# Middle phase of an FFT convolution: the inverse's two blocks together, one period later

## The chip, the cores and the metric

The kernel runs on one core of a Trainium2 chip. The metric is the device time of one execution in microseconds. The engines are TensorE (PE; its weight loads appear as PEld), VectorE (DVE), ScalarE (ACT), GpSimd (POOL) and SyncE (SP, which here only issues DMAs).

## The reference

For a batch of 4, a sequence of 12800 and 128 channels, in float32: a filter comes from a small network on position embeddings, times an exponential window; the product `x * v` is convolved with it along the sequence by FFT; the result times `x` goes through a causal convolution of five taps, a sigmoid gate and two 128x128 projections.

```python
h_filt = (np.maximum(pos_emb @ w1, 0.0) @ w2) * window
u = x * v
y = np.fft.irfft(np.fft.rfft(u, n=2*S, axis=1) * np.fft.rfft(h_filt, n=2*S, axis=0)[None], n=2*S, axis=1)[:, :S]
x = x * y
gate = 1 / (1 + np.exp(-causal_conv5(x, conv_w)))
out = (gate * (x @ w_val)) @ w_out
```

## The kernel before

The sequence is cut into J = 2 blocks of 6400 = N1 x N2 = 100 x 64 points, and the transform is done in two stages. The first phase transforms along the 100 (index `k1` afterwards) and writes `a_u` to memory. The middle phase takes one `k1` after the other, two at a time (a pair p of 0 to 49): it transforms along the 64, multiplies by the filter's spectrum, and does the first stage of the inverse, whose result `c_y` goes to memory. The last phase finishes the inverse, and does the gate and the projections.

The change is in the middle phase alone (lines 398 to 431). Its order is written out by hand: each engine does its work in the order of the code, and waits where a result, or a buffer, is not there yet. Turn p of the loop touches three pairs:

- `load_pair(p + 2)` issues the loads on SP (L354 for a table of weights, once per four pairs, and L359 for the signal). The tiles come from a pool `ld` of six buffers, where a load waits until the buffer's last reader is done.
- `spectrum(.., 1, 0)` and `(.., 1, 1)` of pair p: TensorE, L341, two matmuls each, 64 columns of the array wide ("column tiles"), into `z_ps`, a ring of four PSUM banks that the filter uses too.
- `times` (VectorE, L346) multiplies spectra by the filter: `va` and `vb` (2048 wide) and `vc` and `vd` (1024 wide).
- `inverse` (TensorE, L369) of pair p-1, for block 0 from `va` and for block 1 from `vc`, four matmuls each, with a contraction of 64 rows of the array ("row tiles"), into `c_ps`, two buffers. ScalarE copies each (L376), and after block 1 issues the two stores of `c_y` (L379).
- `start_pair(p + 1)` makes the filter of the next pair (TensorE L328, ScalarE L333 to L335). `first` and `second` are that pair's two spectra of block 0, for `va` and `vb` of the next turn.
- The add of L419 (VectorE) adds half of pair p-1's `va` to its `vc`; `inverse` of block 1 reads the sum.
- Three sums on GpSimd end the turn: L428 (`va[0:2] += vb[0:2]`), L429 (`vc += vd`), L430 (`va[2:4] += vb[2:4]`).

So in turn p VectorE does `va`, `vb`, the add for p-1, `vc`, `vd`. The add needs L429 and L430 of the turn before. L428 needs `vb` of its own turn, L429 needs `vd`. A spectrum's bank in `z_ps` is free again when VectorE has read it: `first` waits for the `vb` before, `second` for the `vc` before, and the pair of block 1 for the `vd` before and for ScalarE's copies of the filter.

Of the kernel before, what the change touches and what calls it, by code (L numbers as in the profile page):

```python
# [105 lines left out]
def tile_longconv_gate(  # L106
# [56 lines left out]
    def load():  # L163
        return ld.tile([128, 2048], F32, name="ld")
# [149 lines left out]
    with tc.tile_pool(name="p2", bufs=1) as p2, tc.tile_pool(name="ps2", bufs=1, space=PSUM) as ps2:  # L314
        BD = B * D
        NP = N1 // 2
        PG = KG // 2
        half = [slice(h * N2, (h + 1) * N2) for h in range(2)]

        def bank():  # L320
            return ps2.tile([128, BD], F32, name="z_ps", bufs=4)

        def filter_pair(p):

            h_ps = bank().rearrange("p (c e) -> p c e", c=2)
            for c in range(2):
                for h in range(2):
                    nc.tensor.matmul(  # L328
                        out=h_ps[half[h], c], lhsT=ag[:, 2 * p + h].rearrange("p j e -> p (j e)")[:, half[c]],
                        rhs=w2bd.rearrange("p j d -> p (j d)"), start=True, stop=True)  # L330
            h_sb = p2.tile([128, 2, J, 2, D], F32, name="h_sb2", bufs=3)
            src = h_ps.rearrange("p c (j d) -> p c j d", j=J)
            nc.scalar.copy(out=h_sb[:, 0].rearrange("p j c d -> p c j d"), in_=src)  # L333
            nc.scalar.activation(h_sb[:, 1, :, 0], src[:, 1], AF.Copy, scale=-1.0)
            nc.scalar.copy(out=h_sb[:, 1, :, 1], in_=src[:, 0])  # L335
            return h_sb

        def spectrum(a2, wk, j, c):
            z = bank()
            for h in range(2):  # L340
                nc.tensor.matmul(out=z[half[h]], lhsT=wk[:, h, half[c]], rhs=a2[:, h, j], start=True, stop=True)  # L341
            return z

        def times(out, z, h_sb, n):

            nc.vector.tensor_tensor(  # L346
                out, z.rearrange("p (b d) -> p b d", d=D).unsqueeze(1).to_broadcast([128, n, B, D]),
                h_sb.unsqueeze(2).to_broadcast([128, n, B, D]), op=ALU.mult)

        def load_pair(p):  # L350
            if p % PG == 0:
                n_p = min(PG, NP - p)
                wt = load().rearrange("p (k c e) -> p k c e", k=PG, c=4)
                nc.sync.dma_start(out=wt[:, 0:n_p], in_=t_w[:, p:p + n_p])  # L354
                weights.append(wt)
            a2 = load().rearrange("p (k j e) -> p k j e", k=2, j=J)
            step = 1 if p == 0 else 2
            for i in range(0, 2, step):
                nc.sync.dma_start(  # L359
                    out=a2[:, i:i + step].rearrange("p k j e -> p k (j e)"),  # L360
                    in_=a_u[2 * p + i:2 * p + i + step].rearrange("k c n j b d -> (c n) k (j b d)"))
            return a2, weights[-1][:, p % PG]

        def inverse(p, j, vt):
            wk = loaded[p][1]
            c_ps = ps2.tile([128, 2, BD], F32, name="c_ps", bufs=2)
            for c in range(2):
                for h in range(2):
                    nc.tensor.matmul(  # L369
                        out=c_ps[:, h], lhsT=wk[half[h], 2 + c], rhs=vt[half[h], c].rearrange("p b d -> p (b d)"),  # L370
                        start=(c == 0), stop=(c == 1))
            if j == 0:
                c_sb = p2.tile([128, 2, J, B, D], F32, name="c_sb", bufs=2)
                outs[p] = c_sb
            c_sb = outs[p]
            nc.scalar.copy(out=c_sb[:, :, j].rearrange("p h b d -> p h (b d)"), in_=c_ps)  # L376
            if j == J - 1:
                for h in range(2):
                    nc.scalar.dma_start(  # L379
                        out=c_y[:, 2 * p + h].rearrange("j p b d -> p j (b d)"),  # L380
                        in_=c_sb[:, h].rearrange("p j b d -> p j (b d)"))

        weights, loaded, outs = [], {}, {}
        filt_p, z0, v_p = {}, {}, {}
        AHEAD = 2

        def start_pair(p):
            filt_p[p] = filter_pair(p).rearrange("p s j c d -> p s (j c) d")

        def first(p):  # L390
            z0[p, 0] = spectrum(*loaded[p], 0, 0)

        def second(p):
            z0[p, 1] = spectrum(*loaded[p], 0, 1)

        with tc.manual_schedule():
            for p in range(-1, NP + 1):
                now, nxt, old = 0 <= p < NP, p + 1 < NP, 0 <= p - 1  # L400
                for q in range(AHEAD + 1) if p < 0 else (p + AHEAD,):
                    if q < NP and q not in loaded:
                        loaded[q] = load_pair(q)
                if now:
                    h = filt_p.pop(p)
                    z10 = spectrum(*loaded[p], 1, 0)
                    z11 = spectrum(*loaded[p], 1, 1)
                    va = p2.tile([128, 2 * J, B, D], F32, name="va", bufs=3)
                    vb = p2.tile([128, 2 * J, B, D], F32, name="vb", bufs=2)
                    times(va, z0.pop((p, 0)), h[:, 0], 2 * J)  # L410
                    times(vb, z0.pop((p, 1)), h[:, 1], 2 * J)
                if old:
                    oa, oc = v_p.pop(p - 1)
                    inverse(p - 1, 0, oa)
                if nxt:
                    start_pair(p + 1)
                    first(p + 1)
                if old:
                    nc.vector.tensor_tensor(oc, oc, oa[:, 2:4], op=ALU.add)  # L419
                    inverse(p - 1, 1, oc)  # L420
                if nxt:
                    second(p + 1)
                if now:
                    vc = p2.tile([128, 2, B, D], F32, name="vc", bufs=3)
                    vd = p2.tile([128, 2, B, D], F32, name="vd", bufs=2)
                    times(vc, z10, h[:, 0, 0:2], 2)
                    times(vd, z11, h[:, 1, 0:2], 2)
                    nc.gpsimd.tensor_tensor(va[:, 0:2], va[:, 0:2], vb[:, 0:2], op=ALU.add)  # L428
                    nc.gpsimd.tensor_tensor(vc, vc, vd, op=ALU.add)  # L429
                    nc.gpsimd.tensor_tensor(va[:, 2:4], va[:, 2:4], vb[:, 2:4], op=ALU.add)  # L430
                    v_p[p] = va, vc
# [234 lines left out]
```

## Time and profile before

| | us |
|---|---|
| Median of 3 runs | 1285.75 |
| Lowest and highest | 1273.37, 1292.47 |
| The profiled execution's time | 1290.03 |
| Its span, first to last instruction | 1288.2 |
| First phase | 0 to about 400 |
| Middle phase | about 400 to 850 |
| Last phase | about 850 to 1288 |

Over the span TensorE is busy for 1174.3 us (91%), VectorE for 1014.1 (79%), GpSimd for 867.4 (67%) and ScalarE for 629.6 (49%). Times in the rows of the timeline are the start in us from the span's start and the duration in us; in brackets stands how long the engine had been idle, and what ended that. In rows of groups stand the count, the busy time in us and the mean in ns, then the idle time before them. "x" and a number is how many instructions a row holds. A float32 matmul of the program appears as two instructions in the trace. TensorE's ends are modelled, so TensorE's times are best read from start to start.

### The profile page before, as it was taken

Reading aid. Unit: us, or ns where it says so; the run is one execution under the profiler, and the core shown is the slowest. Engines: PE = TensorE matmul, PEld = TensorE weight load, DVE = VectorE, ACT = ScalarE, POOL = GpSimd, SP = SyncE. Lnnn points to the kernel's source line nnn. Section 1 sums busy time; section 2 is a strip of 40 time slices with the busy share of each in tenths; the row PEclk is TensorE's granted clock in tenths of the full one; section 3 lists DMA queues with packets and bytes.
Section 4 is the critical chain, followed back from the end, with each engine's and each line's share of the span. In section 5 each row is a group of like instructions: output and inputs, shape, how many; then the busy total and the mean of one; then the engine's idle time right before and its main releaser. Section 6 shows DMA issues by size and latency. Waiting matters only on the chain.

```text
span 1288.2 us, 16767 instructions
## 1 busy us (share of the span) xinstructions
PE 1174.3 (91%) x5544; PEld 572.7 (44%) x5544; DVE 1014.1 (79%) x1130; ACT 629.6 (49%) x1064; POOL 867.4 (67%) x346
## 2 busy tenths in 40 slices
PE   4869999978777899999999999989999999999996
PEld 3557776766543233333333333353344444444432
DVE  5856233797655999999999999902999899999897
ACT  3324454677533233333333333304677677667664
POOL 3324233444543689999999999913898898898790
PEclk8979999988978999999999999986999999999999
DMA  9999878889988577788777777645888988999942
GB/s 244 293 298 311 240 238 270 275 259 304 297 260 306 199 263 282 275 286 293 279 278 278 276 276 258 246 142 154 250 270 269 287 255 274 285 272 268 285 142 102
DMA packets 152254, 332.95 MB, mean 258 GB/s; under 512 B 12446, under 2 KB 64714, under 8 KB 150634
## 3 DMA queue, kind: packets, MB, share of 16 engines
q1 hardware_dynamic: 104256, 226.13, 57.8%
q10 hardware_dynamic: 47914, 105.76, 22.7%
q8 instruction: 45, 0.74, 0.2%
q14 instruction: 39, 0.32, 0.1%
HBM read 200.77 MB, written 131.07 MB: 258 GB/s over the span
## 4 chain that ended last, share of the span: by engine, by line
PE 66%; DMA 16%; DVE 8%; issue 3%; POOL 3%; ACT 3%; SPq 1%; ACTq 0%; DVEq 0%; POOLq 0%
PE c_ps L369 14%; PE z_ps L341 13%; PE sd L503 8%; DMA ld<-in_v_dram 7%; PE o_ps L564 7%; PE fp L282 7%; DMA a_u<-st 6%; PE v_ps L554 5%; PE tp L517 4%; PE z_ps L328 3%; DVE gt L545 3%; PE ap L222 2%; PE ap L221 2%; PE o_ps L589 2%; DVE vc L419 1%
## 5 line engine op out<-in xcount | busy, mean ns | idle before, releaser
L530 POOL TENSOR_TENSOR ext<-yr,ld 128x400 f32<-128x400 f32 x120 | 301.6, 2514 | 60.4 <-DVE yr L528 40.5
L259 POOL TENSOR_TENSOR u_lo<-u_t,u_hi 100x1024 fp32r<-100x1024 f32 x64 | 160.0, 2503 | 236.1 <-ACT u_hi L258 212.2
L545 DVE SCALAR_TENSOR_TENSOR gt<-ext,cw,gt 128x1600 f32<-128x1600 f32 x128 | 242.7, 1896 | 0.9 <-ACT gt L542 0.8
L376 ACT COPY c_sb<-c_ps 128x1024 f32<-128x1024 f32 x100 | 101.2, 1012 | 278.4 <-PE c_ps L369 278.4
L341 PE MATMUL z_ps<-ld 128*64 128x512 f32 x800 | 195.3, 607 | 7.7 <-DMA ld<-a_u 6.5
L428 POOL TENSOR_TENSOR va<-va,vb 128x1024 f32<-128x1024 f32 x50 | 156.9, 3138 | 37.0 <-DVE vb L346 36.9
L282 PE MATMUL fp<-u_hi,fwd_hi 100*100 100x512 f32 x256 | 116.9, 456 | 57.5 <-ACT st L285 24.7
L503 PE MATMUL sd<-ld,inv 100*64 100x512 f32 x512 | 146.1, 645 | 2.4 <-DMA ld<-c_y 2.4
L287 DVE COPY st<-fp 100x512 f32<-100x512 f32 x128 | 85.3, 685 | 65.6 <-PE fp L282 57.9
L346 DVE TENSOR_TENSOR vb<-z_ps,h_sb 128x2048 f32<-128x2048 f32 x50 | 114.5, 2291 | 24.6 <-ACT c_sb L376 24.0
L564 PE MATMUL o_ps<-gd,wout 128*128 128x400 f32 x256 | 119.5, 548 | 13.8 <-DVE gd L559 9.4
L429 POOL TENSOR_TENSOR vc<-vc,vd 128x1024 f32<-128x1024 f32 x50 | 118.2, 2365 | 18.6 <-DVE vd L346 13.7
L257 DVE TENSOR_TENSOR u_t<-ld 100x1024 f32<-100x1024 f32 x64 | 86.2, 1348 | 51.7 <-POOL u_lo L259 42.3
L346 DVE TENSOR_TENSOR va<-z_ps,h_sb 128x2048 f32<-128x2048 f32 x50 | 114.1, 2281 | 10.9 <-PE z_ps L341 10.9
L510 ACT COPY sd_sb<-sd 128x512 f32<-128x512 f32 x128 | 75.8, 592 | 88.5 <-PE sd L503 73.6
L430 POOL TENSOR_TENSOR va<-va,vb 128x1024 f32<-128x1024 f32 x50 | 118.4, 2368 | 0.0
L369 PE MATMUL c_ps<-vc,ld 64*128 64x512 f32 x400 | 102.5, 631 | 11.0 <-DVE vc L419 10.6
L282 PE MATMUL fp<-u_hi,fwd_lo 100*100 100x512 f32 x256 | 108.8, 425 | 0.0
L554 PE MATMUL v_ps<-ext,wval 128*128 128x400 f32 x256 | 107.1, 500 | 0.0
L285 ACT COPY st<-fp 100x512 f32<-100x512 f32 x128 | 70.8, 592 | 73.2 <-PE fp L282 44.2
L341 PEld LDWEIGHTS z_ps<-ld 128*64 128x64 f32 x800 | 54.6, 138 | 114.2 <-issue 85.8
L258 ACT CAST u_hi<-u_t 100x1024 fp32r<-100x1024 f32 x64 | 68.2, 1067 | 74.0 <-PE fp L282 31.8
(78 smaller groups left out, 1962.0 us busy)
## 6 DMA issues: line engine op xcount, KB each, us to landing
c_y<-c_sb ACTq DMA_DIRECT2D x100, 512.0 KB
ld<-a_u SPq DMA_DIRECT2D x49, 1024.0 KB
ld<-c_y SPq DMA_DIRECT2D x128, 384.0 KB
ld<-in_xt_dram SPq DMA_DIRECT2D x32, 800.0 KB
out_dram<-o_sb ACTq DMA_DIRECT2D x32, 800.0 KB
ld<-in_x_dram SPq DMA_DIRECT2D x64, 384.0 KB
ld<-in_v_dram SPq DMA_DIRECT2D x64, 384.0 KB
a_u<-st ACTq DMA_DIRECT2D x64, 384.0 KB
```

The source lines that it names most:

```text
L259: nc.gpsimd.tensor_tensor(lo, u_t, hi.bitcast(F32), op=ALU.subtract)
L282: nc.tensor.matmul(out=fp, lhsT=w[:, c], rhs=d[:, b:b + 2], start=(k == 0), stop=(k == 2))
L341: nc.tensor.matmul(out=z[half[h]], lhsT=wk[:, h, half[c]], rhs=a2[:, h, j], start=True, stop=True)
L346: nc.vector.tensor_tensor(out, z.rearrange("p (b d) -> p b d", d=D).unsqueeze(1).to_broadcast([128, n, B, D]), h_sb.unsqueeze(2).to_broadc ...
L369: nc.tensor.matmul(out=c_ps[:, h], lhsT=wk[half[h], 2 + c], rhs=vt[half[h], c].rearrange("p b d -> p (b d)"), start=(c == 0), stop=(c == 1))
L428: nc.gpsimd.tensor_tensor(va[:, 0:2], va[:, 0:2], vb[:, 0:2], op=ALU.add)
L430: nc.gpsimd.tensor_tensor(va[:, 2:4], va[:, 2:4], vb[:, 2:4], op=ALU.add)
L503: nc.tensor.matmul(out=sd[c * N2:(c + 1) * N2], lhsT=inv[:, c], rhs=ct[c][:, r * B * D:(r + 1) * B * D], start=True, stop=True)
L530: nc.gpsimd.tensor_tensor(e[:, r0 + r], yr, xr, op=ALU.mult)
L545: nc.vector.scalar_tensor_tensor(gt, rows(t, k), cw[:, k:k + 1], gt, op0=ALU.mult, op1=ALU.add)
L554: nc.tensor.matmul(out=v_ps, lhsT=wval, rhs=rows(t)[:, r * ROW:(r + 1) * ROW], start=True, stop=True)
L564: nc.tensor.matmul(out=o_ps, lhsT=wout, rhs=gd, start=True, stop=True)
```

## The change

Both inverses of a pair stand together, in the turn after the one where the add was made, so two turns behind the pair's `va` and `vc`. `second` follows `first` at once. The add stays in its turn, now in a line of its own (L422). The loop has one turn more.

```diff
-            for p in range(-1, NP + 1):
-                now, nxt, old = 0 <= p < NP, p + 1 < NP, 0 <= p - 1
+            for p in range(-1, NP + 2):
+                now, nxt = 0 <= p < NP, p + 1 < NP
...
                     times(va, z0.pop((p, 0)), h[:, 0], 2 * J)
                     times(vb, z0.pop((p, 1)), h[:, 1], 2 * J)
-                if old:
-                    oa, oc = v_p.pop(p - 1)
-                    inverse(p - 1, 0, oa)
+                if p - 2 >= 0:
+                    oa, oc = v_p.pop(p - 2)
+                    inverse(p - 2, 0, oa)
+                    inverse(p - 2, 1, oc)
                 if nxt:
                     start_pair(p + 1)
                     first(p + 1)
-                if old:
+                    second(p + 1)
+                if 0 <= p - 1 < NP:
+                    oa, oc = v_p[p - 1]
                     nc.vector.tensor_tensor(oc, oc, oa[:, 2:4], op=ALU.add)
-                    inverse(p - 1, 1, oc)
-                if nxt:
-                    second(p + 1)
```

On TensorE, in the middle of the phase, the numbers in the names are those of the buffers. Before, one turn and a half, from a `second` and the two spectra of block 1 on: each inverse stands alone between spectra (`va_5003` and `vc_5038` are of one pair, and L328 is the filter).

```order
L341 MATMUL z_ps_5035<-ld_4945,ld_4843 64x512 x2
L341 MATMUL z_ps_5049<-ld_4945,ld_4843 64x512 x2
L341 MATMUL z_ps_5052<-ld_4945,ld_4843 64x512 x2
L369 MATMUL c_ps_5059<-va_5003,ld_4843 128x512 x4
L328 MATMUL z_ps_5066<-w2bd_72,ag_95 64x256 x4
L341 MATMUL z_ps_5075<-ld_4995,ld_4843 64x512 x2
L369 MATMUL c_ps_5079<-vc_5038,ld_4843 128x512 x4
L341 MATMUL z_ps_5087<-ld_4995,ld_4843 64x512 x2
L341 MATMUL z_ps_5099<-ld_4995,ld_4843 64x512 x2
L341 MATMUL z_ps_5102<-ld_4995,ld_4843 64x512 x2
```

The same place now, from the two spectra of block 1 on (`va_4988` and `vc_5023` are the pair that was `va_5003` and `vc_5038`):

```order
L341 MATMUL z_ps_5034<-ld_4930,ld_4828 64x512 x2
L341 MATMUL z_ps_5037<-ld_4930,ld_4828 64x512 x2
L369 MATMUL c_ps_5044<-va_4938,ld_4828 128x512 x4
L369 MATMUL c_ps_5051<-vc_4973,ld_4828 128x512 x4
L328 MATMUL z_ps_5059<-w2bd_72,ag_95 64x256 x4
L341 MATMUL z_ps_5068<-ld_4980,ld_4828 64x512 x2
L341 MATMUL z_ps_5071<-ld_4980,ld_4828 64x512 x2
L341 MATMUL z_ps_5084<-ld_4980,ld_4828 64x512 x2
L341 MATMUL z_ps_5087<-ld_4980,ld_4828 64x512 x2
L369 MATMUL c_ps_5094<-va_4988,ld_4828 128x512 x4
L369 MATMUL c_ps_5101<-vc_5023,ld_4828 128x512 x4
```

The two inverses have moved together and behind a turn's spectra, and the `second` that stood behind `c_ps<-vc` stands right behind `first`, in front of both.

On ScalarE, one turn before: the copy of block 0, the filter's three copies, the copy of block 1, the stores (`c_sb` is the tile that is stored, `h_sb` the filter).

```order
L376 COPY c_sb<-c_ps 128x2x512
L333 COPY h_sb_3959<-z_ps 128x2x2x128
L334 ACTIVATE h_sb_3959<-z_ps 128x2x128
L335 COPY h_sb_3959<-z_ps 128x2x128
L376 COPY c_sb<-c_ps 128x2x512
L379 DMA c_y<-c_sb 128x2x512 x2
```

And now:

```order
L376 COPY c_sb<-c_ps 128x2x512 x2
L379 DMA c_y<-c_sb 128x2x512 x2
L333 COPY h_sb_4054<-z_ps 128x2x2x128
L334 ACTIVATE h_sb_4054<-z_ps 128x2x128
L335 COPY h_sb_4054<-z_ps 128x2x128
```

Both copies and the stores stand ahead of the filter's copies. On VectorE, GpSimd and SP the order is what it was; VectorE's add only has another line number.

## The prediction

> **What bounds the kernel now.** I read the table of stretches first, then the middle phase's groups by form, then its timeline, a fast and a slow period of it apart, then the chain of waits where the one becomes the other. The columns of the stretches are length, then busy time of TensorE, its weight loads, VectorE, ScalarE, GpSimd, then the granted TensorE clock, DMA share and GB/s.
>
> ```profile
> core 0: us, PE busy (x) PEld busy (x) DVE busy (x) ACT busy (x) POOL busy (x), PEclk, DMA share, GB/s
> ...
> 422.00:464.00 42.00, 35.18 (x150) 11.64 (x148) 40.33 (x21) 11.79 (x20) 28.09 (x13) 0.92 0.56 191
> 464.00:836.00 372.00, 372.00 (x1766) 128.73 (x1762) 347.97 (x221) 139.16 (x220) 349.05 (x133) 1.00 0.78 277
> ```
>
> From 464 to 836 us TensorE is busy for 372.00 of 372.00 us at full clock: it bounds the phase there. From 422 to 464 it is not, and VectorE is (40.33 of 42.00). The groups by form of these two stretches, 464 to 836 first, show what differs. The add of L419 (VectorE) takes 1.22 us in the one and 3.37 us in the other, and GpSimd's sum of L428 takes 3.23 us and 2.35 us:
>
> ```profile
> L428 POOL TENSOR_TENSOR va<-va,vb 128x1024 f32<-128x1024 f32 x45 | 145.1, 3225 | 18.4 <-DVE vb L346 18.4
> ...
> L346 DVE TENSOR_TENSOR vb<-z_ps,h_sb 128x2048 f32<-128x2048 f32 x44 | 100.8, 2292 | 24.0 <-ACT c_sb L376 24.0
> ...
> L419 DVE TENSOR_TENSOR vc<-vc,va 128x1024 f32<-128x1024 f32 x45 | 54.8, 1217 | 0.0
> ```
>
> ```profile
> L419 DVE TENSOR_TENSOR vc<-vc,va 128x1024 f32<-128x1024 f32 x4 | 13.5, 3372 | 1.5 <-POOL va L430 1.5
> ...
> L428 POOL TENSOR_TENSOR va<-va,vb 128x1024 f32<-128x1024 f32 x4 | 9.4, 2350 | 0.0
> ```
>
> Whichever of the two starts second is held up by the other. The timeline (start, duration, engine, line) of a slow period and a fast one shows which starts first:
>
> ```profile
> 442.93 2.36 POOL L428 TENSOR_TENSOR va<-va,vb 128x1024 f32<-128x1024 f32 x1
> 442.95 3.41 DVE L419 TENSOR_TENSOR vc<-vc,va 128x1024 f32<-128x1024 f32 x1 [0.17 <-POOL va L430]
> ...
> 446.29 1.21 DVE L346 TENSOR_TENSOR vc<-z_ps,h_sb 128x1024 f32<-128x1024 f32 x1
> ...
> 447.42 1.21 DVE L346 TENSOR_TENSOR vd<-z_ps,h_sb 128x1024 f32<-128x1024 f32 x1
> ...
> 448.56 2.27 DVE L346 TENSOR_TENSOR va<-z_ps,h_sb 128x2048 f32<-128x2048 f32 x1
> 448.71 2.37 POOL L429 TENSOR_TENSOR vc<-vc,vd 128x1024 f32<-128x1024 f32 x1 [3.43 <-DVE vd L346]
> ...
> 450.75 2.28 DVE L346 TENSOR_TENSOR vb<-z_ps,h_sb 128x2048 f32<-128x2048 f32 x1
> 451.05 2.35 POOL L430 TENSOR_TENSOR va<-va,vb 128x1024 f32<-128x1024 f32 x1
> ...
> 453.36 2.35 POOL L428 TENSOR_TENSOR va<-va,vb 128x1024 f32<-128x1024 f32 x1
> 453.43 3.36 DVE L419 TENSOR_TENSOR vc<-vc,va 128x1024 f32<-128x1024 f32 x1 [0.40 <-POOL va L430]
> ```
>
> ```profile
> 649.45 1.22 DVE L419 TENSOR_TENSOR vc<-vc,va 128x1024 f32<-128x1024 f32 x1
> 649.67 3.23 POOL L428 TENSOR_TENSOR va<-va,vb 128x1024 f32<-128x1024 f32 x1 [0.41 <-DVE vb L346]
> ...
> 651.71 1.22 DVE L346 TENSOR_TENSOR vd<-z_ps,h_sb 128x1024 f32<-128x1024 f32 x1
> ...
> 653.00 2.37 POOL L429 TENSOR_TENSOR vc<-vc,vd 128x1024 f32<-128x1024 f32 x1
> ...
> 655.32 2.37 POOL L430 TENSOR_TENSOR va<-va,vb 128x1024 f32<-128x1024 f32 x1
> ...
> 655.67 2.29 DVE L346 TENSOR_TENSOR vb<-z_ps,h_sb 128x2048 f32<-128x2048 f32 x1 [0.55 <-ACT c_sb L376]
> 657.88 1.22 DVE L419 TENSOR_TENSOR vc<-vc,va 128x1024 f32<-128x1024 f32 x1
> ```
>
> There is a ring through both engines: add, `vc`, `vd` on VectorE, then L429 (needs `vd`) and L430 on GpSimd, then the next add (needs L430's result). L428 needs only `vb`.
>
> Slow: `vb` ends at 450.75 + 2.28 = 453.03, before L430 ends at 451.05 + 2.35 = 453.40. So L428 stands ready behind L430 and follows it at once (453.36); the add, which had to hear of L430, starts at 453.43, too late, and takes 3.36. The ring costs 453.43 − 442.95 = 10.48.
>
> Fast: `vb` was held for 0.55 and ends at 657.96, after L430 ends at 657.69. The add follows `vb` on its own engine at 657.88 and wins. The period is 657.88 − 649.45 = 8.43, TensorE's.
>
> From add to L430's end the fast ring takes 657.69 − 649.45 = 8.24, and with the 0.03 from L430's end to a waiting add (453.40 to 453.43) 8.27. So the fast order lasts only while something keeps `vb` at a pace of 8.27 or slower. Now TensorE does, with 8.43.
>
> How the kernel got from slow to fast is in the chain of waits in order of time:
>
> ```profile
> 453.43 3.38 DVE vc L419
> 456.81 0.14 issue
> 456.94 2.85 PE c_ps L369 x8
> 459.79 3.52 PE z_ps L341 x12
> 463.30 1.92 PE c_ps L369 x8
> ```
>
> The long add held `c_ps<-vc` on TensorE; TensorE's clock had dropped in its pause (the stretch's 0.92), so these two groups took 2.85 and 3.52 in place of 1.92 (the chain's third group) and 2.73 (worked out below), 1.7 more in all. `second` stood behind that `c_ps`, so `vb` came late, and the order tipped.
>
> **The change, part by part.** TensorE's part first; these rows give its period:
>
> ```profile
> 646.04 2.79 PE L341 MATMUL z_ps<-ld 128*64 128x512 f32 x12
> ...
> 646.95 0.14 PEld L341 LDWEIGHTS z_ps<-ld 128*64 128x64 f32 x2 [0.29 <-issue]
> ...
> 647.38 0.14 PEld L341 LDWEIGHTS z_ps<-ld 128*64 128x64 f32 x2 [0.28 <-ACT c_sb L376]
> ...
> 648.77 1.99 PE L369 MATMUL c_ps<-va,ld 64*128 64x512 f32 x8
> ...
> 650.68 1.08 PE L328 MATMUL z_ps<-w2bd,ag 128*64 128x256 f32 x8
> ...
> 652.56 1.99 PE L369 MATMUL c_ps<-vc,ld 64*128 64x512 f32 x8
> ```
>
> A pass of 512 columns takes 647.38 − 646.95 = 0.43. Three spectra are six passes, 2.58, and take 648.77 − 646.04 = 2.73; an inverse is four, 1.72, and takes 1.91; filter and `first` are worth four, 1.72, and take 1.88. So each run of one tile shape costs 0.15 to 0.19 beyond its passes. There are four runs per period (column, row, column, row) and two afterwards: 0.34 saved per period by these rows, TensorE 8.43 − 0.34 = 8.09. The saving is bounded by nothing (if the excess belongs to each group) and 0.38.
>
> *The saving* is worth nothing unless the period can fall. VectorE's own chain allows it: 8.43 − 0.55 = 7.88. The ring does not: 8.27 at best. I cost the best case at 8.43 − 8.27 = 0.16 per period.
>
> *The order.* `second` moves ahead of the inverse, and the add's result is now read one period later. Then nothing holds `vb`: it follows `va` at once, as in the slow rows (450.75 − 448.56 = 2.19), and TensorE's 8.09 is quicker than 8.27. From a fast period `vb` then gains 0.18 on L430 each time, and after one or two periods L428 is ready first. That is the slow ring, 10.4.
>
> *The start.* It need not even fall into it: the phase starts there. The first `va`, `vb` and add stand behind the same work as before, and the change takes away the way out. In the slow ring `second` is released by `vc` (its bank), at 446.29 + 1.21 − 442.95 = 4.55 after the add; it needs 0.86, and `vb` reads it at 450.75 − 442.95 = 7.80, so it has about 2.3 to spare. Then `vd` releases the two other spectra (5.68), and two spectra, both inverses, filter and `first` (1.72 + 3.44 + 1.72 + about 0.34) end at 12.9; the next `va` starts at 10.48 + 5.61 = 16.1, 3.2 to spare. To tip the order TensorE must further eat `vb`'s lead of 0.37: 2.7 late or more. The clock's drop made it 1.7 late.
>
> *The copies.* ScalarE copies both blocks back to back before the filter's three copies. It is busy 139.16 of 372, and `va` has the 3.2 above: nothing. If `va` were delayed it would help, by tipping the order.
>
> *The loads.* The weights are read one period longer, so one load in four pairs waits a period longer and has some two periods' lead in place of three. A load by its row on the page
>
> ```profile
> ld<-a_u SPq DMA_DIRECT2D x49, 1024.0 KB
> ```
>
> is 1.05 MB, 3.8 us at the 277 GB/s above, against 16 us or more: nothing. SP's queue keeps its order, with the loads behind that one waiting on later events anyway.
>
> *The end.* One more turn at the end: the last add still waits for L429 and L430, and the inverse of pair 48 falls in that wait. Nothing.
>
> The sum, against the profiled execution's 1290.03 (span 1288.2), itself 4.3 above the median of 1285.75. Of the 50 adds, the first 49 make 48 periods. They run from 422.11 to 834.98, the last to 843.22:
>
> ```profile
> 422.11 3.36 DVE L419 TENSOR_TENSOR vc<-vc,va 128x1024 f32<-128x1024 f32 x1 [0.53 <-POOL va L430]
> ...
> 834.98 1.22 DVE L419 TENSOR_TENSOR vc<-vc,va 128x1024 f32<-128x1024 f32 x1
> ...
> 843.22 1.23 DVE L419 TENSOR_TENSOR vc<-vc,va 128x1024 f32<-128x1024 f32 x1 [4.76 <-POOL va L430]
> ```
>
> Three slow periods, 422.11 to 453.43, make 10.44 each. 48 × 10.44 = 501.1 in place of 412.9: +88.2. The step to the last add is the same ring, 10.44 in place of 843.22 − 834.98 = 8.24: +2.2. Together +90: **1380 us**, slower by 7%.
>
> The Trainium skill, "SBUF — State Buffer", section "Who interferes with whom", says that a VectorE instruction with two SBUF inputs contends with a GpSimd instruction that reads SBUF, and that whichever issues first blocks the other for its whole length. The trace agrees on who waits, not quite on how long: by the rule the add would follow L428's end, 442.93 + 2.36 + 1.22 = 446.51, and it ended at 442.95 + 3.41 = 446.36. By the Trainium skill's rule alone each period would be 0.15 longer and the time 1387; the row decides.
>
> **Rivals.** *VectorE keeps winning* (not slower). The add starts first although L430 has just ended. For it: 45 adds of the profile did. Against it: in them `vb` ended after L430, and where it did not (four adds) GpSimd won each time, once by 0.02. It gives 44 × 0.16 = 7 less, 1283, with the slow start kept, and 48 × 8.27 = 397 in place of 412.9, 1274, without. It decides if `vb` ends less than about 0.1 before L430: the add starts 0.03 after L430's end, L428 0.14 after `vb`'s where GpSimd is free (649.67 − 649.45 = 0.22 behind the add, which starts 657.96 − 657.88 = 0.08 before `vb`'s end).
>
> *Tipping to and fro.* The dropped clock, or a late load, makes TensorE over 2.7 late every few periods, followed by one or two fast ones. Four slow and two fast: (4 × 10.44 + 2 × 8.27) / 6 = 9.72, 48 × 9.72 = 467, +54 and +2 at the end: 1346. Against it: 1.7 is the lateness seen.
>
> *Only TensorE counts.* If the ring could run at 8.09: 44 × 0.34 = 15 less, 1275, and with the slow start gone (4 × 2.01 more) 1267. Against it: 8.27 is made of durations.
>
> *The excess is per group, nothing saved.* TensorE stays at 8.43. The slow ring doesn't need the saving, so this gives 1290 only if the order tips once, and then stays.
>
> For the third rival, the Trainium skill's "TensorEngine Tiling (Array Packing)", section "Key Properties", says that a change of tiling mode drains TensorE. The excess of 0.15 to 0.19 per run agrees with it; it would speak for the change.
>
> **The numbers.** Slow throughout, or nearly: 0.72, 1368 to 1394 (periods of 10.4 to 10.5, and the 19 us from 1273.37 to 1292.47 by which the three times differ, half to each side). To and fro: 0.12, 1310 to 1368. VectorE keeps winning: 0.09. Only TensorE: 0.03. Nothing saved: 0.04. The range takes the first case and the greater part of the second: 1322 to 1396. About 2% is what can be told from no change here. Slower by more: 0.72 and most of 0.12, 0.82. Within: 0.09 + 0.04 and a rest, 0.14. Faster: 0.04, from the two rivals' ends at 1267 and 1274 against a lower bound of 1260.
>
> **What would show it.** Right: the add (now L422) at about 3.4 us for some 49 of 50, L428 at 2.35, adds 10.4 apart, GpSimd idle before L429 until `vd`, TensorE idle about 2 us per period until `vc`, granted clock below 1 in the phase, `vb` without idle time before it. TensorE's busy rows at full clock: two tile-shape runs instead of four, four spectra and the filter in about 4.5 us. Wrong: adds at 1.22 in most periods, or L428 at 3.23; or `vb` or `va` waiting for TensorE in the slow ring, which would mean that my 2.7 was too much.

## The result, and the profile after

The changed kernel takes 1372.59 us (median of 6 runs, 1369.60 to 1375.84) against 1288.53 for the kernel before in the same runs. The ratio is 1.0686, 95% interval 1.0641 to 1.0730: 6.9% slower. The prediction said 1380, within 1322 to 1396.

The profiled execution took 1372.35 us, its span is 1370.6. The stretches of it, with the columns as before:

```profile
core 0: us, PE busy (x) PEld busy (x) DVE busy (x) ACT busy (x) POOL busy (x), PEclk, DMA share, GB/s
...
422.00:464.00 42.00, 33.72 (x150) 11.04 (x146) 40.39 (x21) 10.49 (x16) 28.29 (x13) 0.96 0.52 183
464.00:900.00 436.00, 362.55 (x1674) 123.18 (x1674) 419.40 (x210) 131.75 (x209) 292.10 (x126) 0.98 0.65 226
```

What held from 422 to 464 us before now holds to the end of the phase: VectorE is the busy engine (419.40 of 436), TensorE has 73 us to spare. The groups by form from 422 to 920 us give the same two instructions as before, and TensorE's spectra with the idle time before them:

```profile
L341 PE MATMUL z_ps<-ld 128*64 128x512 f32 x766 | 200.8, 625 | 85.5 <-DVE vc L346 82.8
L422 DVE TENSOR_TENSOR vc<-vc,va 128x1024 f32<-128x1024 f32 x48 | 161.4, 3363 | 19.6 <-POOL va L430 19.6
L429 POOL TENSOR_TENSOR vc<-vc,vd 128x1024 f32<-128x1024 f32 x48 | 113.9, 2373 | 164.5 <-DVE vd L346 164.5
...
L428 POOL TENSOR_TENSOR va<-va,vb 128x1024 f32<-128x1024 f32 x48 | 113.3, 2360 | 0.0
```

All 48 adds there take 3.36 us, and L428 2.36. One period of the timeline, from add to add (start, duration, engine, line):

```profile
640.58 2.37 POOL L428 TENSOR_TENSOR va<-va,vb 128x1024 f32<-128x1024 f32 x1
640.67 3.37 DVE L422 TENSOR_TENSOR vc<-vc,va 128x1024 f32<-128x1024 f32 x1 [0.41 <-POOL va L430]
...
645.22 3.07 PE L341 MATMUL z_ps<-ld 128*64 128x512 f32 x12 [1.86 <-DVE vc L346]
...
648.42 2.27 DVE L346 TENSOR_TENSOR vb<-z_ps,h_sb 128x2048 f32<-128x2048 f32 x1
648.71 2.35 POOL L430 TENSOR_TENSOR va<-va,vb 128x1024 f32<-128x1024 f32 x1
650.04 1.88 PE L369 MATMUL c_ps<-vc,ld 64*128 64x512 f32 x8
...
651.02 2.36 POOL L428 TENSOR_TENSOR va<-va,vb 128x1024 f32<-128x1024 f32 x1
651.10 3.37 DVE L422 TENSOR_TENSOR vc<-vc,va 128x1024 f32<-128x1024 f32 x1 [0.40 <-POOL va L430]
...
651.86 1.08 PE L328 MATMUL z_ps<-w2bd,ag 128*64 128x256 f32 x8
```

`vb` ends at 650.69, L430 at 651.06; L428 starts before the add by 0.08, and the add is held up. The period is 651.10 − 640.67 = 10.43. `second` (645.22) waits 1.86 for `vc`, which frees its bank, and is still ready long before `vb`.

### The profile page after: what moved, and what is told of

Read it like the earlier page. It is cut to its first block, busy times and chain, and to the rows that moved or that the text cites. A ratio compares the mean times of both kernels' runs of the same rounds, so it can differ in the third digit from the quotient of the medians.

```text
span 1370.6 us, 16722 instructions
## 1 busy us (share of the span) xinstructions
PE 1177.6 (86%) x5544; PEld 572.9 (42%) x5544; DVE 1110.2 (81%) x1130; ACT 630.1 (46%) x1064; POOL 825.1 (60%) x346
## 4 chain that ended last, share of the span: by engine, by line
PE 39%; DVE 23%; POOL 17%; DMA 13%; issue 5%; ACT 3%; SPq 1%; ACTq 0%; DVEq 0%; POOLq 0%
DVE vc L422 9%; PE sd L503 8%; POOL vc L429 8%; POOL va L430 8%; PE fp L282 7%; PE o_ps L564 6%; DMA a_u<-st 5%; PE v_ps L554 5%; DVE vd L346 4%; DVE vc L346 4%; DMA ld<-in_v_dram 4%; PE tp L517 4%; DVE gt L545 2%; PE ap L221 2%; PE ap L222 2%
## 5 line engine op out<-in xcount | busy, mean ns | idle before, releaser
L341 PE MATMUL z_ps<-ld 128*64 128x512 f32 x800 | 211.1, 628 | 95.2 <-DVE vc L346 82.8
L429 POOL TENSOR_TENSOR vc<-vc,vd 128x1024 f32<-128x1024 f32 x50 | 118.6, 2372 | 167.9 <-DVE vd L346 167.9
L422 DVE TENSOR_TENSOR vc<-vc,va 128x1024 f32<-128x1024 f32 x50 | 166.0, 3320 | 24.7 <-POOL va L430 24.7
L341 PEld LDWEIGHTS z_ps<-ld 128*64 128x64 f32 x800 | 50.8, 139 | 222.2 <-DVE vc L346 126.3
L503 PE MATMUL sd<-ld,inv 100*64 100x512 f32 x512 | 140.4, 617 | 2.3 <-DMA ld<-c_y 2.3
L257 DVE TENSOR_TENSOR u_t<-ld 100x1024 f32<-100x1024 f32 x64 | 89.9, 1406 | 50.3 <-POOL u_lo L259 38.2
L428 POOL TENSOR_TENSOR va<-va,vb 128x1024 f32<-128x1024 f32 x50 | 118.0, 2360 | 19.4 <-DMA ld<-a_u 19.4
L430 POOL TENSOR_TENSOR va<-va,vb 128x1024 f32<-128x1024 f32 x50 | 118.1, 2361 | 0.0
L282 PE MATMUL fp<-u_lo,fwd_hi 100*100 100x512 f32 x256 | 101.5, 427 | 1.5 <-POOL u_lo L259 1.5
```

The lines of the kernel that those rows point to most:

```text
L282: nc.tensor.matmul(out=fp, lhsT=w[:, c], rhs=d[:, b:b + 2], start=(k == 0), stop=(k == 2))
L503: nc.tensor.matmul(out=sd[c * N2:(c + 1) * N2], lhsT=inv[:, c], rhs=ct[c][:, r * B * D:(r + 1) * B * D], start=True, stop=True)
```

## The experiments

The theory is the ring of the prediction: add, `vc`, `vd`, L429, L430, add, with L428 in the add's way where it starts first. The rivals are a bank theory (TensorE's new waits for `vc` and `vd`, which free the banks of `z_ps`, set the period) and a later-inverse theory (reading products and weights a turn later costs the time).

**Without L428.** The changed kernel without the one sum.

```diff
-                    nc.gpsimd.tensor_tensor(va[:, 0:2], va[:, 0:2], vb[:, 0:2], op=ALU.add)
```

> The changed kernel without GpSimd's sum of L428; this leaves the second half of the products out of the first half of va, so block 0 of the output lacks them. Ring theory (L428 starts ahead of the add and holds it up; the ring add, vc, vd, L429, L430, add sets the period): the add falls from 3.37 to 1.22 us, adds stand 8.27 apart in place of 10.43, time about 1267. Bank theory (TensorE's waits for vc and vd, which free the z_ps banks, set the period): L428 is in nobody's way, adds stay 10.4 apart, time about 1372. Later-inverse theory (the two turns between a product and its inverse cost the time): also about 1372.

Measured: 1275.60 us, and 1278.30 for the kernel before beside it. Two adds of its timeline:

```profile
635.12 1.23 DVE L422 TENSOR_TENSOR vc<-vc,va 128x1024 f32<-128x1024 f32 x1 [0.30 <-POOL va L429]
...
643.42 1.23 DVE L422 TENSOR_TENSOR vc<-vc,va 128x1024 f32<-128x1024 f32 x1 [0.18 <-POOL va L429]
```

The add takes 1.23 and the period is 8.30; 8.27 was expected. (The line of the last sum is now L429.) This kernel has the changed kernel's order on TensorE, its waits for banks and its later inverse, so neither rival can account for the 10.43. The time is 9 above the expected one, in a single run; 6 of that lie ahead of the first add, which starts at 427.76 us in place of the changed kernel's 421.65.

**Without the add, in both kernels.** The add of L422, or L419, is left out.

```diff
-                    nc.vector.tensor_tensor(oc, oc, oa[:, 2:4], op=ALU.add)
```

> The changed kernel without VectorE's add; this leaves half of va out of block 1. Ring theory: no ring is left, TensorE's own work is the bound, turns of about 8.10 us (8 passes of 0.43 for the inverses and 10 for the rest, and two runs with an excess of 0.2 and 0.15), time about 1258. VectorE and GpSimd alone would allow 6.7 and 7.1. Bank theory: the waits for vc and vd remain, turns stay well above 9. If the excess belongs to each group and not to the change of tile shape: 8.43, time about 1277.

> The kernel before without VectorE's add; this leaves half of va out of block 1. Ring theory: TensorE bound at 8.43 us a turn, and the four slow periods of the start are gone: about 1278. The difference to the changed kernel without the add is then the saving on TensorE alone: 0.34 a turn, 16 us in all; 0 if the excess belongs to each group.

Measured: 1253.06 and 1269.86 us. The filter's matmuls of two turns in a row, of the changed kernel and of the one before:

```profile
640.39 1.08 PE L328 MATMUL z_ps<-w2bd,ag 128*64 128x256 f32 x8
...
648.47 1.08 PE L328 MATMUL z_ps<-w2bd,ag 128*64 128x256 f32 x8
```

```profile
638.16 1.08 PE L328 MATMUL z_ps<-w2bd,ag 128*64 128x256 f32 x8
...
646.59 1.08 PE L328 MATMUL z_ps<-w2bd,ag 128*64 128x256 f32 x8
```

These turns take 8.08 and 8.43 us. Over 45 turns, from 438.06 to 803.09 us and from 444.19 to 823.69, the means are 8.11 and 8.43. So with the ring gone the change saves 0.32 to 0.35 per turn on TensorE, 15 to 17 us in 48 turns. The two times, of one run each, differ by 16.8; that they fit so closely is in part chance, for runs of one kernel spread by more. A turn with two changes of tile shape fewer is shorter by about what the rows before had shown.

**More work for TensorE.** One of the filter's two matmul pairs is made twice.

```diff
-            for c in range(2):
+            for c in (0, 0, 1):
```

> The changed kernel, with one of the filter's two matmul pairs made twice in each turn, the same result: 0.43 us more of TensorE per turn. Ring theory: nothing changes, adds 10.43 apart, since TensorE has over 2 us to spare in each period: 1372. Bank theory (or any in which TensorE is the bound): 48 times 0.43, 21 us more, 1393.

Measured: 1365.56 us. The adds from 464 to 820 us:

```profile
L422 DVE TENSOR_TENSOR vc<-vc,va 128x1024 f32<-128x1024 f32 x34 | 114.5, 3368 | 13.7 <-POOL va L430 13.7
```

They stand 10.43 apart as before, and TensorE's wait for `vc` is 1.43 us (at 649.42) in place of 1.86. So the 0.43 us per turn disappears in TensorE's spare time. This single run is 7 us quicker than the changed kernel; 6 of these lie ahead of the first add, which starts at 415.37 in place of 421.65.

**GpSimd's sums in another order**, in both kernels.

```diff
-                    nc.gpsimd.tensor_tensor(va[:, 0:2], va[:, 0:2], vb[:, 0:2], op=ALU.add)
-                    nc.gpsimd.tensor_tensor(vc, vc, vd, op=ALU.add)
                     nc.gpsimd.tensor_tensor(va[:, 2:4], va[:, 2:4], vb[:, 2:4], op=ALU.add)
+                    nc.gpsimd.tensor_tensor(va[:, 0:2], va[:, 0:2], vb[:, 0:2], op=ALU.add)
+                    nc.gpsimd.tensor_tensor(vc, vc, vd, op=ALU.add)
```

> The changed kernel, with GpSimd's sums in another order: both sums that need only vb (L428's second half of va first, then its first half) ahead of the one that needs vd. The work is the same. Ring theory: the ring to the next add loses one sum of 2.3 us, so that even a held-up add lets the period fall to 8.1 (3.37 + 2.25 for the add and on to the end of vd, 0.1, 2.37 for the last sum, 0.03), which is also TensorE's 8.1 and just above GpSimd's own 7.1 to 8.0: 8.1 to 8.2 apart, time 1258 to 1265, faster than before by about 2%. Bank theory and later-inverse theory: no change from 1372.

> The kernel before with the same other order of GpSimd's sums. Ring theory: TensorE's 8.43 a turn from the start on, the four slow periods of the start are gone: 8 us less than before, about 1279. Then the change itself is worth some 16 us where the ring does not stand in the way. If the start's slow periods had another cause than the ring, no change.

Measured on the changed kernel: 1258.95 us against 1279.64, ratio 0.9841 with interval 0.9789 to 0.9894. It is the fastest complete version here, 1.6% below the kernel before. Measured on the kernel before: 1303.15 us, ratio 1.0179, interval 1.0118 to 1.0240, so the forecast of a gain was wrong there. The changed kernel's groups from 464 to 820 us, and then the kernel before's VectorE and GpSimd over two periods, show both (the sums' lines are now L428 and L429 for `va`, L430 for `vc`):

```profile
L346 DVE TENSOR_TENSOR va<-z_ps,h_sb 128x2048 f32<-128x2048 f32 x44 | 100.8, 2291 | 8.9 <-ACT h_sb L333 8.5
...
L422 DVE TENSOR_TENSOR vc<-vc,va 128x1024 f32<-128x1024 f32 x44 | 53.9, 1224 | 0.2
```

```profile
640.36 1.21 DVE L419 TENSOR_TENSOR vc<-vc,va 128x1024 f32<-128x1024 f32 x1
...
645.96 2.27 DVE L346 TENSOR_TENSOR vb<-z_ps,h_sb 128x2048 f32<-128x2048 f32 x1
648.49 3.36 DVE L419 TENSOR_TENSOR vc<-vc,va 128x1024 f32<-128x1024 f32 x1 [0.26 <-POOL vc L430]
651.77 1.21 DVE L346 TENSOR_TENSOR vc<-z_ps,h_sb 128x1024 f32<-128x1024 f32 x1
...
656.24 2.27 DVE L346 TENSOR_TENSOR vb<-z_ps,h_sb 128x2048 f32<-128x2048 f32 x1
658.43 1.21 DVE L419 TENSOR_TENSOR vc<-vc,va 128x1024 f32<-128x1024 f32 x1
```

```profile
646.07 2.39 POOL L430 TENSOR_TENSOR vc<-vc,vd 128x1024 f32<-128x1024 f32 x1
648.39 2.38 POOL L428 TENSOR_TENSOR va<-va,vb 128x1024 f32<-128x1024 f32 x1
```

In the kernel before, periods of 8.13 and 9.94 alternate. After a quick add, VectorE has `vb` done at 648.23, before GpSimd's last sum ends at 648.46, so L428 wins and the next add is held up. After a held-up add, VectorE's own chain is the bound: it works without a pause from 648.49 to 658.43, 9.94 us. By then GpSimd is long done, so the next add is quick again. My expectation had the ring through GpSimd (8.1) and left out VectorE's own chain with a held-up add. With a quick add that chain is 645.96 − 640.36 = 5.60 up to `vb`, and 658.43 − 656.24 = 2.19 from there to the next add, 7.79 together; a held-up add takes 3.36 in place of 1.21, which makes 9.94. The mean of 9.04 in place of 8.43 gives 48 × 0.61 = 29 more, less the 8 of the start: 21; measured 23.5.

In the changed kernel the same order happens to run without alternating: `va` waits some 0.2 each turn for the filter's copy on ScalarE, which holds `vb` back just enough, and the adds stand 8.14 apart. In most turns `vb` ends within about 0.1 of the last sum, so the reserve is small. One of the four runs was profiled; that the order held in the other three is inferred from the times, 1253.53 to 1261.57, where alternating would add some 40.

**A single delay.** `second` of pair 12 makes its matmuls eight times.

```diff
-            z0[p, 1] = spectrum(*loaded[p], 0, 1)
+            z0[p, 1] = spectrum(*loaded[p], 0, 1, 8 if p == 12 else 1)
```

> The changed kernel, with second's matmuls of pair 12 made eight times over (6 us of TensorE, once), the same result. Ring theory: vb comes late once, two or three fast periods follow, then the slow ring is back, since TensorE's pace of 8.1 is below the 8.27 that the fast order needs: 45 or more of 50 adds at 3.37, time 1369 to 1374. If either order kept itself up once it is there: fast from pair 13 on, 37 times 2.1 less, about 1300.

Measured: 1379.86 us. The adds around it:

```profile
527.47 3.37 DVE L423 TENSOR_TENSOR vc<-vc,va 128x1024 f32<-128x1024 f32 x1 [0.40 <-POOL va L431]
...
541.44 1.21 DVE L423 TENSOR_TENSOR vc<-vc,va 128x1024 f32<-128x1024 f32 x1
...
551.57 1.22 DVE L423 TENSOR_TENSOR vc<-vc,va 128x1024 f32<-128x1024 f32 x1
...
559.86 1.23 DVE L423 TENSOR_TENSOR vc<-vc,va 128x1024 f32<-128x1024 f32 x1
...
568.15 3.37 DVE L423 TENSOR_TENSOR vc<-vc,va 128x1024 f32<-128x1024 f32 x1 [0.29 <-POOL va L431]
```

Late once, three quick adds, and back. TensorE's pace of 8.08 does not keep up the fast order. The 6 us above the expected 1374 lie behind the last add, where this run took 445.0 us and the changed kernel's profile has 437.9.

**The delay and a slower TensorE.** The same, with the doubled filter pair of above.

> The changed kernel with both: second of pair 12 made eight times over, once, and one of the filter's matmul pairs made twice in each turn (0.43 us more of TensorE per turn). Ring theory: TensorE's pace is now 8.53, above 8.27, so once vb has come late the fast order stays: adds of 1.22 us and 8.5 apart from pair 13 on, 37 times 1.9 less, about 1305, although TensorE has more to do than in any run of the changed kernel. Any theory in which TensorE's work costs time: 1372 or more.

Measured: 1370.04 us; the expectation failed. The fast order stayed for four adds, and was lost at the fifth. VectorE's `vb` and add, and ScalarE's issue of the two stores, of this kernel:

```profile
558.55 1.21 DVE L423 TENSOR_TENSOR vc<-vc,va 128x1024 f32<-128x1024 f32 x1
...
565.48 2.28 DVE L347 TENSOR_TENSOR vb<-z_ps,h_sb 128x2048 f32<-128x2048 f32 x1
567.67 1.22 DVE L423 TENSOR_TENSOR vc<-vc,va 128x1024 f32<-128x1024 f32 x1
...
573.45 2.28 DVE L347 TENSOR_TENSOR vb<-z_ps,h_sb 128x2048 f32<-128x2048 f32 x1
575.96 3.36 DVE L423 TENSOR_TENSOR vc<-vc,va 128x1024 f32<-128x1024 f32 x1 [0.23 <-POOL va L431]
```

```profile
552.54 0.89 ACTq L380 DMA_DIRECT2D c_y<-c_sb  x2
...
561.06 1.49 ACTq L380 DMA_DIRECT2D c_y<-c_sb  x2
...
569.64 0.89 ACTq L380 DMA_DIRECT2D c_y<-c_sb  x2
```

The stores at 561.06 took 0.60 longer to issue. The filter's copies stand behind them, `va` and `vb` behind those, and the add came at 9.12 in place of 8.51. TensorE had not been late, so the next `vb` was in time again, and ended before the last sum (L431 in this kernel). The ring needs 8.27 from add to add and TensorE gave 8.51: a reserve of 0.24, against a delay of 0.61. Two runs bear on this. One gives TensorE still more to do, all of the filter's matmuls twice (`for c in (0, 1, 0, 1)`):

> As the run with the one-time delay and 0.43 us more of TensorE per turn, but with 0.86 us more (all of the filter's matmuls twice): TensorE's pace is 8.93. There the fast order was lost when ScalarE's stores took 1.49 in place of 0.89 us to issue and vb came 0.6 late, once, against a reserve of about 0.3. Now the reserve is 0.7. Ring theory: the fast order stays from pair 13 on, adds of 1.22 us and 8.9 to 9.0 apart, 37 times 1.5 less than 1372 and 4 for the delay: about 1322. If the late stores were not the cause, or TensorE's pace not the condition: back to 10.43, 1372.

The other leaves the 0.43, and takes the stores out of the way, by issuing them behind the filter's copies:

```diff
                     second(p + 1)
+                if p - 2 >= 0:
+                    store(p - 2)
```

> As the run with the one-time delay and 0.43 us more of TensorE per turn, but ScalarE issues the stores behind the filter's copies of the same turn, not ahead of them. If the long issue of the stores was what lost the fast order there: it stays, 8.5 apart from pair 13 on, about 1305. If not: back to 10.43, 1368 to 1374.

Measured: 1323.13 and 1301.96 us. Late in the phase, the adds of the first and then of the second:

```profile
813.88 1.22 DVE L423 TENSOR_TENSOR vc<-vc,va 128x1024 f32<-128x1024 f32 x1
...
822.83 1.21 DVE L423 TENSOR_TENSOR vc<-vc,va 128x1024 f32<-128x1024 f32 x1
```

```profile
807.00 1.22 DVE L426 TENSOR_TENSOR vc<-vc,va 128x1024 f32<-128x1024 f32 x1
...
815.51 1.22 DVE L426 TENSOR_TENSOR vc<-vc,va 128x1024 f32<-128x1024 f32 x1
```

The fast order stays in both, 8.95 and 8.51 apart. Neither shows what a delay of 0.6 would have done there, since no issue of the stores was as long once the order was fast: the longest took 1.17 us in the first and 1.16 in the second. What they show is smaller. In the first, behind an issue of 1.12 (at 673.55), the add came after 9.03 and the order held; in the second, behind the issue of 1.16 (at 631.47), it came after 8.51 as always, so the moved stores are out of its path. That the long issue lost the order in the run before rests on that run's rows alone. Against the changed kernel's 1372.59 the first is 49 us quicker, although all that was done to it is to give TensorE more work in each turn and to make it late once.

**Parts of the change.** In the kernel before, `second` alone is moved ahead of the add and the inverse of block 1:

```diff
+                if nxt:
+                    second(p + 1)
                 if old:
                     nc.vector.tensor_tensor(oc, oc, oa[:, 2:4], op=ALU.add)
                     inverse(p - 1, 1, oc)
-                if nxt:
-                    second(p + 1)
```

> The kernel before with one part of the change alone: second made ahead of the add and of block 1's inverse, which stay in their turn. TensorE keeps four runs of tile shapes and 8.43 a turn. Ring theory: no matmul that vb waits for stands behind the add any more, so nothing tips the slow start: adds of 3.37 us, 10.43 apart for all of the phase, time about 1372. If the two inverses together, or a turn later, cost the time: as before, 1278 to 1290.

In the changed kernel, `second` is put behind the two inverses, which stay together and a turn later:

```diff
+                if nxt:
+                    start_pair(p + 1)
+                    first(p + 1)
                 if p - 2 >= 0:
                     oa, oc = v_p.pop(p - 2)
                     inverse(p - 2, 0, oa)
                     inverse(p - 2, 1, oc)
                 if nxt:
-                    start_pair(p + 1)
-                    first(p + 1)
                     second(p + 1)
```

> The changed kernel with second behind the two inverses, which stay together and a turn later: column and row runs still alternate once per turn. The inverses don't wait for the add of their turn, so second behind them is no brake. Ring theory: slow throughout, 10.43 apart, about 1372. If it is second's place behind an inverse, whichever, that counts: fast from the start's end on, 8.3 to 8.5 apart, about 1285.

Measured: 1374.09 and 1372.47 us, with 1283.56 for the kernel before. The adds from 422 to 920 us, of the one and the other:

```profile
L421 DVE TENSOR_TENSOR vc<-vc,va 128x1024 f32<-128x1024 f32 x48 | 161.4, 3362 | 19.6 <-POOL va L430 19.6
```

```profile
L423 DVE TENSOR_TENSOR vc<-vc,va 128x1024 f32<-128x1024 f32 x49 | 164.4, 3356 | 19.7 <-POOL va L431 19.7
```

Moving `second` ahead does the whole damage by itself, with TensorE's four runs kept. And `second` behind inverses is no cure where these don't wait for the add of the same turn. The kernel before got to its fast order by way of that one wait: add, inverse of block 1, `second`, `vb`. The wait was not enough by itself, for it stands in each of that kernel's four slow periods, of which only the last tipped. One row for each, with the columns of the stretches:

```profile
422.10:432.50 10.40, 7.85 (x38) 2.49 (x34) 10.02 (x5) 2.50 (x6) 6.97 (x4) 1.00 0.53 187
432.50:442.95 10.45, 8.43 (x36) 2.64 (x32) 10.12 (x5) 2.86 (x5) 7.01 (x5) 0.84 0.49 191
442.95:453.40 10.45, 10.13 (x52) 3.56 (x50) 10.07 (x5) 3.37 (x6) 7.02 (x4) 1.00 0.65 213
453.40:463.90 10.50, 8.57 (x36) 2.79 (x34) 10.02 (x5) 2.95 (x5) 6.99 (x3) 0.84 0.54 170
```

The third last column is the granted clock. At 1.00, in the first and the third, `vb` waited for nothing. At 0.84, in the second, `vb` ended at 442.78, still 0.14 before the last sum (442.92); in the fourth it waited 0.45 for TensorE and ended at 464.00, 0.19 after the last sum (463.81). So the wait tipped the order only together with the dropped clock, and had just missed it once. How many slow periods the other runs of the kernel before began with is not known.

## Why the prediction was right

*The ring and its two lengths.* Right: 10.43 with the add at 3.37, and 8.30 without L428, where 10.44 and 8.27 were predicted.

*The saving on TensorE.* 0.34 was predicted, 0.32 to 0.35 measured. It was there, and worth nothing behind the ring, as costed. The rival of the excess per group falls with it.

*The start and the way out.* Right. The first add is held up as before, and none gets free but the last, behind which no sum of GpSimd's follows. `second` starts 645.22 − 640.67 = 4.55 after the add, as was worked out. The run with only `second` moved shows that the place of `second` took the way out, and the run with 0.43 more per turn that TensorE has at least that much to spare.

*The order does not last.* Right in kind: after a delay three adds, not one or two periods' worth, then the slow ring. But "only while something keeps `vb` at a pace of 8.27 or slower" was not enough of a condition. At a pace of 8.5 the order was lost to a single delay of 0.6 that did not come from TensorE. The size of the reserve counts as well, by that run's rows: 0.24 against 0.61. At 8.95, or with the stores moved, the order held, but no delay as long came up there.

*The copies.* "Nothing" was right in the slow ring, though with less to spare than the 3.2 of the prediction: the filter's last copy ends at 644.33 + 0.38 = 644.71 in the period above, and `va` starts at 646.22, 1.5 later. In the fast order ScalarE's stores and copies stand on `va`'s path, as the run that lost it and the reordered sums' 0.2 show.

*Loads and end.* Right: 82.8 of the 85.5 us for which TensorE stood idle before a spectrum end with `vc`, by the group's row above, none with a load, and the last step took 932.68 − 922.31 = 10.37, by these two adds of the changed kernel:

```profile
922.31 3.35 DVE L422 TENSOR_TENSOR vc<-vc,va 128x1024 f32<-128x1024 f32 x1 [0.41 <-POOL va L430]
...
932.68 1.23 DVE L422 TENSOR_TENSOR vc<-vc,va 128x1024 f32<-128x1024 f32 x1 [4.76 <-POOL va L430]
```

*The sum.* 82.3 us were added to the profiled execution, not 90. The 48 periods took 48 × 10.43 = 500.6, 87.8 more, and the last step 2.1 more, as summed. From the last add to the end it took 1370.6 − 932.68 = 437.9 in place of 445.0: 7.1 less, in code that is the same. In the twelve profiles here that have the add, this stretch takes 433.9 to 445.0, and the prediction started from one at the upper end. So the mechanism gave its 90 almost exactly, and the miss of 7 to 8 is the spread of another phase, whose cause is open.

*VectorE keeps winning.* It did not. In all profiles here, each of the 339 held-up adds began 0.02 to 0.10 after a sum of GpSimd's, and `vb` had ended 0.14 or more before the sum that the add waited for. No quick add began while a sum ran. Where a further sum came next on GpSimd and `vb` had ended 0.04 or less before that sum, as at 776.64 in the changed kernel with the sums reordered, the add started first. The prediction's "less than about 0.1" lies between the two.

*The dropped clock.* The granted clock after was 0.98 from 464 to 900 us, not much below 1, so its drops were too few to matter, and the rival of tipping to and fro came to nothing.

## What to carry to other kernels

Where two engines each wait for the other once per turn, look in the timeline at which of two contending instructions starts first and what decides it: a wait that seems to be in the way may be what keeps the good order. A saving on the busiest engine should be costed against every ring through the others, and against the state that the loop starts in. Taking one sum out of the ring, by another order of three lines on GpSimd, let most of the saving through (8.14 us per turn in place of 8.43), with a small reserve; in the kernel before, the same order cost time.

## What the runs showed of the hardware

A held-up add lost about 2.15 us to an instruction that had started 0.02 to 0.10 us sooner, every time. GpSimd, with its next instruction ready, followed its own last one at once, while VectorE started some 0.03 after that one's end, so it never won; it did where that next instruction was not ready yet. The Trainium skill, "SBUF — State Buffer", section "Who interferes with whom", states the rule of first come; the runs add that in a loop a tenth of a microsecond decides which of two steady periods a kernel has, 8.4 or 10.4.

Not expected was that issuing two stores occupies ScalarE's queue for 0.89 us in most turns and now and then for 1.49 to 1.91 (1.49 at 561.06 in the run that lost the fast order, 1.91 at 745.45 in the kernel before with the sums reordered), and that so small a delay could cost a loop its faster order. It need not: behind an issue of 1.57 at 761.82, the changed kernel with the sums reordered had one period of 8.75, and kept its order.
